# Two linear-attention and two windowed-attention layers on one core: rows of the second linear layer normalised earlier, more buffers in a preparation, transpositions spread out, and a value tile moved in attention's first segment

## The chip, the cores and the metric

The kernel runs on one core of a Trainium2 chip. The metric is the device time of one execution in microseconds. TensorE (PE in the profile) multiplies matrices and transposes by multiplying with an identity; VectorE is DVE, ScalarE is ACT, GpSimd is POOL, and SP is the engine that issues most DMAs. Each engine works through its own queue in order.

## The reference

```python
x = A_x                                            # 2048 rows of 512 floats
x = x + A(layernorm(x)); x = x + B(layernorm(x))
x = x + A(layernorm(x)); x = x + B(layernorm(x))   # the same weights again

def A(x, wqkv, w_phi, wo):           # linear attention, 32 heads of 16
    q, k, v = heads(x @ wqkv)
    f = lambda t: concat(softmax(t @ w_phi), softmax(-(t @ w_phi)))   # 32 features
    o = f(q) @ (f(k).T @ v) / (f(q) @ sum(f(k)) + 1e-6)
    return merge(o) @ wo

def B(x, wq, wk, wv, wo, beta):      # attention in 4 segments of 512 rows, with a memory M, z
    for s in range(4):
        a_dot = softmax(q_s @ k_s.T / 4 + causal_mask) @ v_s
        a_mem = phi(q_s) @ M / (phi(q_s) @ z + 1e-6)      # phi(t) = t + 1 or exp(t)
        o_s = sigmoid(beta) * a_mem + (1 - sigmoid(beta)) * a_dot
        M, z = M + phi(k_s).T @ v_s, z + sum(phi(k_s))
    return merge(o) @ wo
```

## The kernel before, in words

Everything is fp32; where a projection needs precision, an operand is split into a high part and a remainder (names `hh`/`hl`, `oh`/`ol`, `ta`, `e`, `w`) and three matmuls replace one. ACT copies the high part out of PSUM, VectorE subtracts it for the remainder. One PSUM tag, `g`, with three buffers, takes all projections and transpositions; `lg` and `mx` (one buffer each) take the scores and the scores for the row maxima, `pv` the weighted values.

The order of each engine's instructions is the order of the Python program: every call through `dve`, `act`, `pool`, `sync` and every matmul is bound to the one before it (`Ordered`, `held`). The order is made by generators that are advanced one step at a time. While `loose` is set, an instruction keeps behind the ordered ones before it, but later ones need not keep behind it.

A linear layer has two passes. `pass1` goes over four segments of 512 rows in the order `SEGS` = 1, 2, 3, 0: rows are normalised (`norm_T`: statistics `moments`, then `guard` and `root`, `refine`, then `normal`, then `columns`, which transposes a tile of 128 rows into `hT`), then projected to k, q and v; features of k are multiplied with v into `kva`; q goes to DRAM. `go` yields some 36 steps a segment, and the list `plan` says at which steps the next segment's columns, its value tile and the statistics of the segment after it are advanced. `pass2` (144 steps) reads q back, multiplies its features with the sum, and makes the layer's output.

During the first layer's `pass1`, `prepare` runs one step to one: it loads the weights of the output projections and of attention, splits them (`act.copy` for the high part, `pool.tensor_tensor` for the rest) and stores both parts to DRAM. It does 32 quarter pieces and then 12 whole ones. `rows` keeps loads of 128 rows (`xr`) ahead, `parts` takes the tiles for the parts (`oh`, `ol`).

An attention layer is `steps`. A slot is one step k; five slots make one half group m of 4 heads; 8 m make a segment. In every slot one step of `attend` (scores, exponentials) and one of `maxima` (scores again, row maxima; it runs `LEAD` = 9 slots ahead) is done. All else is written by hand in tables: "2.3 fin ln~" means at half group 2, slot 3, `finish` and one step of the next segment's normalisation (`~`: its VectorE part one slot later). "/2" does two steps of the four. `BEFORE` is the same for the slots before 0: eight projections (q, k, v) of the first segment. `FIRST` is the table of the first segment, `GAPS` of the second and third, `LAST` and `FINAL` of the fourth. In `LAST` "v", "ln", "n" and "N" advance the next linear layer's `pass1`; what is left of it runs after attention. `aside` holds what is to be done at attention's very end.

Attention begins while `pass2` ends. `A20` steps of `pass2` are done with `opening` in between (first loads, normalisation of the first segment), then `steps` starts at slot `BEGIN` = -25 and does the rest of `pass2` (`side`) spread over the slots from `MAXIMA` to 1: in each slot until the work done, in estimated nanoseconds of TensorE, reaches its share of `LEFT`.

Of the kernel before, what the change touches and what calls it, by code (L numbers as in the profile page):

```python
# [8 lines left out]
F32R = mybir.dt.float32r  # L9
# [17 lines left out]
OT = 6  # L27
TA = 8
OO = 3
MT = 2  # L30
PV = 1
G = 3
# [2 lines left out]
LEAD = 9  # L35
FINAT = 8
PAUSE, DONE = object(), object()
LEFT = 25000
BEGIN = -25
MAXIMA = -9  # L40
A20 = 105
PREP = 3
EVERY = 2
NEXT = (3, 2, 3, 2)
SEGS = (1, 2, 3, 0)
# [2 lines left out]


FIRST = """  # L50
0.1 max k2/2       | 0.3 k2~           | 0.4 m0
1.1 max q3/2       | 1.3 fin q3~       | 1.4 t1 k3/1
2.1 max m1 k3      | 2.3 fin ln~       | 2.4 ln~ ln~
3.3 fin q0+/2      | 3.0 w
3.1 max ln~        | 3.4 q0+~ t2
4.1 max k0+/2 load | 4.3 fin k0+/1     | 4.4 k0+ m2
5.0 n              | 5.3 fin q1+/2 n
5.1 max v0+        | 5.4 q1+~ t3
6.1 max a0+ v1+    | 6.2 n             | 6.3 a0+ fin k1+/2
# [37 lines left out]
6.1 max out~       | 6.3 fin           | 6.4 pt~  # L97
7.1 p pt~          | 7.3 fin p pt      | 7.4 p pt
"""
BEFORE = {-25: "q0", -23: "v0", -21: "k0", -20: "load", -19: "v1",  # L100
          -18: "n", -17: "v2 n", -16: "n", -15: "n n", -14: "q1 n", -13: "n", -12: "k1 n", -11: "n", -10: "v3 n",
          -4: "max q2~", -1: "t0"}


# [1 line left out]
def interleave_kernel(ctx, tc, x_in, a_wqkv, a_wphi, a_wo, b_wq, b_wk, b_wv, b_wo, b_beta,  # L106
# [29 lines left out]
    aside = [None]  # L136
# [163 lines left out]
    def prepare():  # L300


        yield from constants()
        for _ in range(PREP):
            yield
        jobs = [(src, kc) for src in (b_wq, b_wk, a_wo, b_wv, b_wo) for kc in range(NC)]
        asked = []

        def rows():

            while jobs and len(asked) < 3:
                src, kc = jobs.pop(0)
                asked.append(T2("xr", 3))
                sync.dma_start(out=asked[-1], in_=src[kc * P : (kc + 1) * P, :])
            return asked.pop(0)

        def parts():
            return rows(), T2("oh", OO, F32R), T2("ol", OO, F32R)

        def pieces():  # L320
            for m in range(2):
                for kc in range(NC):
                    tiles = parts()
                    for e in range(2):
                        for r in range(2):
                            views = [tiles[0].rearrange("p (c f r e d) -> p e r c d f", c=NC, f=2, r=2, e=2)]
                            views += [t.rearrange("p (c f e d r) -> p e r c d f", c=NC, e=2, f=2, r=2)
                                      for t in tiles[1:]]
                            keep = [wqk[m][:, :, a, kc, :] for a in range(2)] if e and r else ()
                            yield [v[:, e, r] for v in views], keep, tiles[1:]  # L330
            for key in ("awo", "bwv", "bwo"):
                kept[key] = [dtile((P, NC, D), nm(key)) for _ in range(2)]
                for kc in range(NC):
                    tiles = parts()
                    yield tiles, [k[:, kc, :] for k in kept[key]], tiles[1:]

        def turn_by_turn():
            loose[0] = True
            piece = next(todo, None)
            loose[0] = False  # L340
            return piece

        copied, stored, todo = None, None, pieces()
        for piece in chain(iter(turn_by_turn, None), (None, None)):
            loose[0] = True
            if stored:
                _, keep, tiles = stored
                for k, t in zip(keep, tiles):
                    dma(k, t.rearrange("p (c x) -> p c x", c=NC) if len(k.shape) == 3 else t)
            if copied:  # L350
                (raw, hi, lo), _, _ = copied
                pool.tensor_tensor(out=lo, in0=raw, in1=hi.bitcast(F32), op=SUB)
            if piece:
                (raw, hi, _), _, _ = piece
                act.copy(hi, raw)
            loose[0] = False
            copied, stored = piece, copied
            for _ in range(EVERY):
                yield
# [131 lines left out]
        dve.tensor_tensor(out=t, in0=p[:, :, :, 0:DH], in1=rb, op=MUL)  # L491
        eng.tensor_tensor(out=out, in0=out, in1=t, op=ADD)

    def v_tile(hT, w, vv, tag):
        v = sp.tile([P, 4, VROW], F32, tag="v", bufs=2, name=nm("v"))
        vv[:] = [v]
        pool.memset(v[:, :, 0 : H * VW].rearrange("p t (h e) -> p t h e", e=VW)[:, :, :, DH : DH + 1], 1.0)
        pool.memset(v[:, :, H * VW : VROW], 0.0)
        for t in range(4):
            po = PS(*tag)  # L500
            yield from tok_proj(po, hT, t, w)
            act.copy(v[:, t, 0 : H * VW].rearrange("p (h e) -> p h e", e=VW)[:, :, 0:DH],
                           po.rearrange("p (h e) -> p h e", e=DH))
            yield
# [80 lines left out]
    class LayerA:  # L585
# [68 lines left out]
        def pass1(self, first):  # L654
            hTs, vv = [], []

            def upcoming(n):

                h = []
                spare = ("e8" if first else "w8") if n % 2 else None  # L660
                return h, norm_T(self.xsrc, SEGS[n], h, spare, slow=True, off=True)

            if first:
                wq, wk, wv, upc = self.first(hTs, vv, upcoming)
            else:
# [9 lines left out]
                    next(vt)  # L675
                    yield
                wk = load_w("awk", None, "e8")
                yield from vt
            self.mmq = [T2("mmq", 2, shape=(P, NT // 2, 2, H)) for _ in range(2)]
            kva = sp.tile([P, 8, 4 * VW], F32, tag="acc", bufs=1, name=nm("kva"))  # L680
            late = None
            for n, s in enumerate(SEGS):
# [53 lines left out]
                    yield  # L736

                if n < NSEG - 1:
                    if n == 0 and not first:
                        upc = upcoming(1)  # L740
                        next(upc[1])
                    hTs, g = upc
                    vv = []
                    if n or first:
                        plan = [(4 + j, g) for j in range(4)]
                        vals, norms = [10 + j * 26 // 16 for j in range(16)], (8, 14, 16, 18, 20, 22, 24, 28, 30, 32, 34)
                    else:
                        plan = [(j, g) for j in (8, 9, 12, 13, 14, 15, 17, 18, 19, 20)]
                        vals, norms = [21 + j * 13 // 16 for j in range(16)], (21, 26, 27, 28, 29, 30, 31, 33, 34, 35, 36)
                    vt = v_tile(hTs, wv, vv, ("g", G))  # L750
                    plan += [(j, vt) for j in vals]
                    if n + 2 < NSEG:
# [24 lines left out]
                    for i, _ in enumerate(go(late)):  # L777
                        if i == 4 and n == 0 and not first:
                            wq = load_w("awq", None, "e8")
                            aside[0].append(lambda: [next(g) for _ in range(4)])  # L780
                        while plan and plan[0][0] <= i:
                            next(plan.pop(0)[1], None)
                        if n == 1 and i % 4 == 0:
                            settle(1)
                        yield
# [84 lines left out]
    class LayerB:  # L870
# [20 lines left out]
        def values(self, s):  # L891

            self.vv[s] = []
            yield from v_tile(self.hT[s], self.wv, self.vv[s], ("g", G))

        def queue_w(self):

# [395 lines left out]
    for i in range(2):  # L1293
# [3 lines left out]
        opening = lb.opening()  # L1297
        for k in range(A20):
            next(a2)
            if k in (6, 9, 12, 18, 24, 30) or k > 41 and k % 3 == 0:  # L1300
                next(opening, None)
        for _ in opening:
            pass
# [32 lines left out]
```

## Time and profile before

| | us |
|---|---|
| median of three runs | 1599.54 |
| lowest and highest | 1596.80, 1601.78 |
| the profiled execution | 1604.31 |
| its span, first to last instruction | 1602.6 |
| busy: PE / DVE / ACT / POOL | 1518.1 / 1130.9 / 785.6 / 651.7 |
| mean granted TensorE clock | 0.983 |

The profile is of one execution. A line of the timeline has the start, the busy time, the engine, the operation with output and inputs, the count of merged instructions, and in brackets the idle time of the engine before it and what ended that. An idle time is a loss only where the engine is the one that sets the pace; here this is TensorE for nearly all of the span. Names of tiles are without buffer numbers; `x` is rows, `st` their statistics, `P` the exponentials or features, `mxs` the maxima. Line 183 is the helper of all matmuls, 187 that of all transpositions, 161 that of all other engines, so lines say little here, and one goes by tiles.

### The profile page before, as it was taken

Reading aid. Unit: us, or ns where it says so; the run is one execution under the profiler, and the core shown is the slowest. Engines: PE = TensorE matmul, PEld = TensorE weight load, DVE = VectorE, ACT = ScalarE, POOL = GpSimd, SP = SyncE. Lnnn points to the kernel's source line nnn. Section 1 sums busy time; section 2 is a strip of 40 time slices with the busy share of each in tenths; the row PEclk is TensorE's granted clock in tenths of the full one; section 3 lists DMA queues with packets and bytes.
Section 4 is the critical chain, followed back from the end, with each engine's and each line's share of the span. In section 5 each row is a group of like instructions: output and inputs, shape, how many; then the busy total and the mean of one; then the engine's idle time right before and its main releaser. Section 6 shows DMA issues by size and latency. Waiting matters only on the chain.

```text
span 1602.6 us, 28186 instructions
## 1 busy us (share of the span) xinstructions
PE 1518.1 (95%) x9856; PEld 1083.3 (68%) x9856; DVE 1130.9 (71%) x3252; ACT 785.6 (49%) x1178; POOL 651.7 (41%) x1006
## 2 busy tenths in 40 slices
PE   7998999988999999999989999998989999999997
PEld 6787887765566666665557888877556666666554
DVE  5654677577778878878554557756788788787783
ACT  5543345325565565565533323343455655655553
POOL 1567555213444544433222336532234444433322
PEclk9998999999999999999988999999999999999999
DMA  4477265534443543535231103735353444444331
GB/s 161 135 260 256 66 198 158 157 99 134 126 112 104 143 99 105 142 94 152 90 129 40 40 20 101 235 105 147 111 170 110 107 136 103 106 112 101 80 102 39
DMA packets 108765, 195.71 MB, mean 122 GB/s; under 512 B 14416, under 2 KB 27856, under 8 KB 107856
## 3 DMA queue, kind: packets, MB, share of 16 engines
q1 hardware_dynamic: 107472, 193.38, 41.2%
q8 instruction: 79, 1.29, 0.4%
q10 hardware_dynamic: 1152, 0.52, 0.1%
q14 instruction: 62, 0.51, 0.1%
HBM read 101.05 MB, written 39.85 MB: 88 GB/s over the span
## 4 chain that ended last, share of the span: by engine, by line
PE 67%; DVE 18%; ACT 5%; issue 5%; POOL 3%; DMA 2%; SPq 0%; ACTq 0%; POOLq 0%; DVEq 0%
PE g L183 38%; DVE mx L161 8%; PE lg L183 8%; PE mx L183 8%; PE g L187 7%; PE pv L183 7%; POOL P L161 2%; ACT tb L161 2%; DVE es L161 2%; ACT P L161 1%; DVE mxs L161 1%; DVE ta L161 1%; DVE mmq L161 1%; ACT x L161 1%; DMA xr<-in 1%
## 5 line engine op out<-in xcount | busy, mean ns | idle before, releaser
L161 DVE CUSTOM_DVE_ANT_0 mx<-mx,mask 128x128 f32<-128x128 f32 (+3 forms) x1024 | 510.9, 499 | 163.2 <-PE mx L183 128.6
L161 ACT ACTIVATE P<-lg 128x1024 f32<-128x1024 f32 x320 | 328.8, 1028 | 178.9 <-PE lg L183 171.1
L161 POOL TENSOR_SCALAR_AFFINE_SELECT P<-P 128x256 f32<-128x256 f32 (+1 forms) x448 | 191.3, 442 | 444.3 <-ACT P L161 443.2
L183 PE MATMUL g<-hh,wqk 128*128 128x512 f32 x512 | 180.3, 407 | 1.0 <-ACT mt L161 0.7
L183 PE MATMUL mx<-e,e 63*128 63x256 f32 (+2 forms) x1024 | 156.2, 362 | 25.8 <-DVE mxs L161 20.2
L183 PE MATMUL lg<-e,e 64*128 64x256 f32 (+2 forms) x1024 | 168.5, 387 | 7.9 <-ACT P L161 7.1
L183 PE MATMUL g<-w,oh 128*128 128x512 f32 x512 | 171.5, 417 | 4.3 <-DVE hl L161 2.5
L183 PE MATMUL pv<-P,v 128*32 128x512 f32 (+3 forms) x2048 | 166.1, 443 | 0.0
L183 PEld LDWEIGHTS lg<-e,e 64*128 64x128 f32 x1024 | 81.2, 184 | 102.7 <-issue 53.9
L183 PE MATMUL g<-w,hh 128*128 128x512 f32 x448 | 145.5, 406 | 1.5 <-ACT tb L161 0.9
L161 DVE DVE_READ_ACCUMULATOR2_ANT mxs<- 128x1 f32 x1024 | 144.8, 141 | 0.0
L183 PEld LDWEIGHTS mx<-e,e 63*128 63x128 f32 x1024 | 83.2, 186 | 74.8 <-DVE mxs L161 55.9
L183 PEld LDWEIGHTS pv<-P,v 128*32 128x32 f32 x2048 | 54.0, 110 | 99.6 <-issue 89.2
L183 PEld LDWEIGHTS g<-hh,wqk 128*128 128x128 f32 x512 | 96.3, 188 | 22.3 <-ACT mt L161 1.1
L183 PEld LDWEIGHTS g<-w,oh 128*128 128x128 f32 x512 | 90.9, 192 | 27.3 <-issue 2.8
L161 POOL TENSOR_SCALAR tb<-tb 128x512 f32<-128x512 f32 x48 | 71.5, 1491 | 82.0 <-ACT tb L161 82.0
L183 PE MATMUL g<-w,ol 128*128 128x512 f32 x256 | 103.0, 402 | 0.0
L183 PE MATMUL g<-hl,wqk 128*128 128x512 f32 x256 | 100.0, 390 | 0.0
L161 ACT COPY v<-g 128x512 f32<-128x512 f32 x64 | 37.6, 587 | 120.1 <-PE g L183 119.8
L161 ACT CAST ta<-g 128x512 fp32r<-128x512 f32 x64 | 37.5, 585 | 117.4 <-PE g L183 117.4
L183 PEld LDWEIGHTS g<-w,hh 128*128 128x128 f32 x448 | 79.8, 189 | 20.3 <-ACT tb L161 2.7
L183 PE MATMUL g<-w,hl 128*128 128x512 f32 x224 | 88.1, 393 | 0.0
(133 smaller groups left out, 2729.5 us busy)
## 6 DMA issues: line engine op xcount, KB each, us to landing
e<-ta SPq DMA_DIRECT2D x384, 128.0 KB
wqk<-wqk SPq DMA_DIRECT2D x64, 512.0 KB
x<-x SPq DMA_DIRECT2D x48, 256.0 KB
xr<-in SPq DMA_DIRECT2D x28, 256.0 KB
pq<-tb SPq DMA_DIRECT2D x24, 256.0 KB
tb<-pq SPq DMA_DIRECT2D x24, 256.0 KB
x<-xr SPq DMA_DIRECT2D x24, 256.0 KB
xr<-x SPq DMA_DIRECT2D x24, 256.0 KB
```

Of the source, the lines that this page charges most:

```text
L161: i = f(*a, **k)
L183: return held(nc.tensor.matmul(*a, **k))
L187: return held(nc.tensor.transpose(*a))
```

## The change

Five things change. In `prepare` up to five row loads run ahead instead of three, into the six buffers `ot` instead of the three of `xr`, and both parts come from the eight buffers `ta1` instead of three each of `oh` and `ol`. In `pass1` of the second linear layer the normalisation of the second segment is begun while the value tiles of the first are projected (in attention's last rows), with its refinement on VectorE instead of GpSimd, and its last steps follow early in the first segment; the steps done at attention's end fall away. In all other segments of `pass1` columns and statistics come at other steps, further apart. At attention's start five more steps of `pass2` come before the slots, the rest begins at slot -14 instead of -9, and the list `STEPS` replaces a rule for when `opening` is advanced. In attention's first segment the last value tile moves behind slot 0, the value tiles are made in the order 0, 3, 1, 2 (in every segment), the product m0 comes a slot later, and the four transposition steps "ln" stand in four slots instead of three.

```diff
-LEFT = 25000
+LEFT = 21700
 BEGIN = -25
-MAXIMA = -9
-A20 = 105
+MAXIMA = -14
+STEPS = (6, 9, 12, 18, 24, 30, *range(42, 91, 3), 93, 100, 102, 109)
+A20 = 110
...
 FIRST = """
-0.1 max k2/2       | 0.3 k2~           | 0.4 m0
-1.1 max q3/2       | 1.3 fin q3~       | 1.4 t1 k3/1
-2.1 max m1 k3      | 2.3 fin ln~       | 2.4 ln~ ln~
-3.3 fin q0+/2      | 3.0 w
-3.1 max ln~        | 3.4 q0+~ t2
-4.1 max k0+/2 load | 4.3 fin k0+/1     | 4.4 k0+ m2
+0.1 max k2/2       | 0.2 v3/2          | 0.3 k2~
+0.4 v3             | 1.1 max m0 q3/2   | 1.3 fin q3~       | 1.4 t1 k3/1
+2.1 max m1 k3      | 2.3 fin ln~       | 2.4 ln~
+3.1 max ln~        | 3.3 fin ln~       | 3.0 w
+3.4 q0+/2 t2       | 4.1 max q0+~ load | 4.3 fin k0+/2     | 4.4 k0+ m2
...
-BEFORE = {-25: "q0", -23: "v0", -21: "k0", -20: "load", -19: "v1",
-          -18: "n", -17: "v2 n", -16: "n", -15: "n n", -14: "q1 n", -13: "n", -12: "k1 n", -11: "n", -10: "v3 n",
+BEFORE = {-25: "q0", -23: "v0", -21: "k0", -20: "load",
+          -18: "n", -17: "v1 n", -16: "n", -15: "n n", -14: "q1 n", -13: "n", -12: "k1 n", -11: "n", -10: "v2 n",
           -4: "max q2~", -1: "t0"}
...
-            while jobs and len(asked) < 3:
+            while jobs and len(asked) < 5:
                 src, kc = jobs.pop(0)
-                asked.append(T2("xr", 3))
+                asked.append(T2("ot", OT))
...
-            return rows(), T2("oh", OO, F32R), T2("ol", OO, F32R)
+            return rows(), T2("ta1", TA, F32R), T2("ta1", TA, F32R)
...
-    def v_tile(hT, w, vv, tag):
+    def v_tile(hT, w, vv, tag, order=range(4)):
...
-        for t in range(4):
+        for t in order:
...
-            def upcoming(n):
+            def upcoming(n, off=True):
...
-                return h, norm_T(self.xsrc, SEGS[n], h, spare, slow=True, off=True)
+                return h, norm_T(self.xsrc, SEGS[n], h, spare, slow=True, off=off)
...
                 wk = load_w("awk", None, "e8")
-                yield from vt
+                upc = upcoming(1, False)
+                next(upc[1])
+                for n, _ in enumerate(vt):
+                    if n > 1:
+                        next(upc[1])
+                    yield
...
-                    if n == 0 and not first:
-                        upc = upcoming(1)
-                        next(upc[1])
                     hTs, g = upc
                     vv = []
-                    if n or first:
-                        plan = [(4 + j, g) for j in range(4)]
-                        vals, norms = [10 + j * 26 // 16 for j in range(16)], (8, 14, 16, 18, 20, 22, 24, 28, 30, 32, 34)
-                    else:
-                        plan = [(j, g) for j in (8, 9, 12, 13, 14, 15, 17, 18, 19, 20)]
-                        vals, norms = [21 + j * 13 // 16 for j in range(16)], (21, 26, 27, 28, 29, 30, 31, 33, 34, 35, 36)
+                    plan = [(j, g) for j in ((0, 2, 4, 4, 8, 9, 11, 13) if n == 0 and not first else (4, 7, 10, 13))]
+                    vals, norms = [10 + j * 26 // 16 for j in range(16)], (14, 20, 22, 24, 26, 27, 28, 31, 33, 34, 35)
...
                             wq = load_w("awq", None, "e8")
-                            aside[0].append(lambda: [next(g) for _ in range(4)])
...
-            yield from v_tile(self.hT[s], self.wv, self.vv[s], ("g", G))
+            yield from v_tile(self.hT[s], self.wv, self.vv[s], ("g", G), (0, 3, 1, 2))
...
-            if k in (6, 9, 12, 18, 24, 30) or k > 41 and k % 3 == 0:
+            if k in STEPS:
                 next(opening, None)
```

## The prediction

> **What bounds the kernel now.** I read the page's slices first, then busy time by windows, then the timeline and the chain of waits where the windows show loss.
>
> ```profile
> PE   7998999988999999999989999998989999999997
> PEclk9998999999999999999988999999999999999999
> 147.39:151.48 4.09, 0.00 (x0) 0.00 (x0) 4.02 (x7) 1.45 (x4) 2.02 (x3) 0.82 0.92 302
> 150.02:160.26 10.24, 8.78 (x36) 8.29 (x37) 2.39 (x4) 1.24 (x2) 7.12 (x6) 0.50 0.66 246
> 832.68:853.16 20.48, 16.86 (x63) 14.45 (x64) 8.82 (x14) 6.12 (x10) 5.51 (x7) 0.50 0.22 64
> 281.88:305.20 23.32, 23.16 (x107) 18.72 (x105) 7.33 (x15) 7.80 (x15) 4.04 (x8) 1.00 0.60 176
> 305.20:352.40 47.20, 42.77 (x233) 32.42 (x232) 36.39 (x109) 15.20 (x25) 8.79 (x9) 0.93 0.38 109
> 352.40:400.70 48.30, 41.57 (x314) 24.99 (x313) 37.79 (x131) 26.89 (x37) 18.10 (x34) 1.00 0.46 132
> ```
>
> (Columns of a window: length; busy PE, PEld, DVE, ACT, POOL; PE clock; DMA share; GB/s.) TensorE is busy 95% of the span and the change alters no matmul, so it can win only idle TensorE time (1602.6 − 1518.1 = 84.5 us) and stretches at half clock. The loss sits where the change works: the weight preparation in the first pass (slice at 120–160), the passage from the first attention layer to the second linear layer (820–880), and the start of each attention layer (305–400; the second, 1093–1190, shows the same waits).
>
> ```profile
> 145.64 0.62 ACT L161 CAST oh<-xr 128x512 fp32r<-128x512 f32 x1 [3.62 <-DMA bwv<-ol]
> 146.49 1.29 POOL L161 TENSOR_TENSOR ol<-xr,oh 128x512 fp32r<-128x512 f32 x1 [0.95 <-DMA bwv<-ol]
> 151.48 6.67 PE L183 MATMUL lg<-v,P 128*128 128x68 f32 x30 [4.09 <-POOL P L161]
> ...
> 832.56 0.70 POOL L161 TENSOR_SCALAR st<-st 128x4 f32<-128x4 f32 x1
> 833.29 2.93 ACT L161 ACTIVATE x<-x,st 128x512 f32<-128x512 f32 x4 [1.03 <-POOL st L161]
> 834.16 1.11 PE L187 MATMUL g<-ident,x 128*128 128x128 f32 x4 [4.12 <-ACT x L161]
> 841.09 1.12 PE L187 MATMUL g<-ident,x 128*128 128x128 f32 x4 [1.96 <-DVE w L161]
> ```
>
> First stall: the preparation's cast sits 3.62 us at the head of ACT's queue waiting on a DMA, the copies behind it reach VectorE late, and TensorE waits 4.09 us for scaled features. Second: rows normalised too late hold TensorE 4.12 and 1.96 us. A half-clock stretch follows each.
>
> **The change, part by part** (minus is a gain).
>
> *More buffers in prepare().* Casts, subtractions and stores stay; five row loads instead of three run ahead, in six buffers instead of three, and four pairs of parts instead of three. The cast at 145.64 needed a row loaded, or a part stored, about 5 us before (the store issued at 140.96 lands at 146.34); pieces come 2.4 us apart, so one or two more pieces of lead cover most of it. On SP a load no longer stands until the subtraction just before it frees its buffer (SP waited 29.2 us for `ol` between 60 and 290); two loads more at the start, 0.5 MB, fall into the slice with DMA share 0.4. Worth: 4.09 idle, plus half of the 8.78 us busy in the half-clock stretch, 4.39: 8.5. Against it: DMA share is 0.92 there, and the last 12 pieces move 9.4 MB in about 36 us, 260 GB/s, where the busiest windows reach 390. Bounds 0 and −8.5; nearer the full amount: **−7.5**.
>
> *Transpositions apart in pass 1.* Columns at steps 4, 7, 10, 13 instead of 4 to 7; waits before such transposes are 1.06 (at 42.39), 1.56 (127.12), 0.97 and 1.59 (876.70, 879.64), 0.95 (923.93): 6.1. Each is a VectorE remainder or an ACT copy behind other work of the same step; three steps (some 4 us) between them should clear half. The later loads (step 14 rather than 8) still stand six steps ahead of their statistics. Bounds −6 and +1: **−3**.
>
> *Second linear layer's rows sooner.* Gain: statistics, root and the refinement (now on VectorE) come before the end of attention. 4.12 + 0.19 + 1.95 idle go, and half of the 16.86 us busy in the half-clock stretch, 8.4: −14.7. Cost: where the statistics are moved to. They stand in VectorE's program at slots 6.3 and 6.4 of the last attention segment, some 790 us, ahead of the weighing of the memory product and of the early projection's remainder `ol`. Their rows come through SP, whose queue there reads
>
> ```profile
> 791.55 0.32 SPq L161 DMA_DIRECT2D tb<-x  x1
> 791.92 3.83 SPq L161 DMA_DIRECT2D e<-awk  x8
> 795.84 2.46 SPq L161 DMA_DIRECT2D x<-x  x4
> 796.00:799.00 3.00, 3.00 (x14) 2.45 (x15) 0.69 (x1) 1.03 (x1) 0.41 (x1) 1.00 0.94 240
> 799.00:802.00 3.00, 3.00 (x30) 1.55 (x28) 0.56 (x1) 2.23 (x4) 0.41 (x2) 1.00 1.04 393
> 802.00:805.00 3.00, 2.71 (x15) 2.19 (x14) 0.68 (x2) 1.29 (x2) 1.83 (x4) 1.00 0.58 214
> ```
>
> The row loads keep their place behind 2 MB of awk, itself behind a load that waited 21.5 us for TensorE; the DMA engines work that off until about 804, so row 0 lands near 802. VectorE, in order, stands from 790.5 until then. Behind it wait the weighing that frees one of three g buffers and the `ol` that the matmul at 795.86 uses third. Statistics cost 0.87 us a row: two rows and 0.9 us of weighing, TensorE goes on at 804.3; two more rows and the 0.56 us `ol`, 806.8. So it idles about 8.4 + 2.1 = 10.5 us it does not idle now; queued behind it are all projections of slot 7.1 on. After idle times of 4 us the trace shows half clock for 10.24 and 20.48 us, elsewhere for 3.41; two windows of 3.41 with TensorE busy cost 3.4. Net −14.7 + 13.9: **−1**; bounds −14.7 (rows there in time) and +4 (three windows, and a microsecond or two for ACT's root before VectorE's refinement). The refinement's six small operations, 0.2 us each, leave POOL for VectorE. The four normalisations (0.80 us each on ACT) and four moments otherwise lie beside work: ACT and VectorE have idle times of 1 to 3 us in every slot there.
>
> The Trainium skill (TensorE: Matmul & The Clock Gate, "What's actually happening") says that one busy window of about 3.4 us restores the full clock; by it the new stall would cost 1.7 instead of 3.4 us of clock, and this term be about −2.5. The trace disagrees for the two stretches of 10.24 and 20.48 us, three and six windows, with TensorE busy 82 to 86% of them.
>
> *Attention's start* (twice). The list STEPS gives the same 24 useful calls as the old rule (up to 93; the later three find the opening finished): nothing. Five steps of pass 2 run before the slots: four transposes 0.60, two products 2.24, half an output projection 1.38: 4.2 us. The rest is spread over 16 slots from −14 instead of 11 from −9, so 5/16 of 21.7 = 6.8 us falls among the projections; a value tile (2.75 us; eight projections take 22.0) leaves them. The dense stage gets +4.2 + 6.8 − 2.75 = +8.2, at full clock. The stage of first maxima (305.20 to 352.40) loses 11.0 us of TensorE work and some 8 us of VectorE's (4.4 us a tile: remainder 0.69, scaling 1.75, weighing 1.3, residual 0.69). Its floors, TensorE 42.77 − 3.4 (two half-clock windows) and VectorE 36.39, then fall to 28.4 each; its slack over the higher floor, 7.8 us, will grow as TensorE's matmuls and VectorE's maxima share one mx buffer and alternate: 38 us, −9.2. Bounds: no saving at all, and −13. The value tile comes back at slots 2 and 4, into gaps of 0.93 + 0.24 + 0.61 + 0.87 us: +1 (0.1 to 2.75). If that cover goes, the whole 2.75 is paid. The memory product, a slot later, has its reader in the next segment. The value order (0, 3, 1, 2) asks for tiles 0 and 3 first, as the weighted product does: nothing. The ln transpositions of segment 0: the gaps from 382 to 393 (3.3 us) lose perhaps 0.5. Per start 8.2 − 9.2 + 1 − 0.5 = −0.5: **−1** for two, bounds −10 and +17.
>
> Sum: −7.5 − 3 − 1 − 1 = −12.5. The profiled execution took 1604.31 (span 1602.6 and 1.7 around it), so 1591.8 in its terms; it stands 4.8 above the median 1599.54, so the median after is **1587.0**.
>
> **The rivals.**
>
> *The rows come in time*: were they loaded before VectorE reaches the statistics, 13.9 us of new stall vanish and the time is 1573. For it: a normalisation asked for earlier is what the edit says. Against it: SP's lines above; nothing ahead of the rows leaves the queue.
>
> *The DMA wait only moves in prepare()*: at 0.92 share more loads in flight make each slower, another cast stops, and the part is worth 0 to −1: 1594. For it: the share; against it: 0.2 to 0.3 of the engines in use between 106 and 117, room to load ahead.
>
> *Slower: the first maxima keep their length.* If the 47.2 us are set by the alternation over the one mx buffer (11 slots of 4.3 us, VectorE busy 77%) and not by the side work, the saving of 9.2 fails and both starts cost 8.2 + 1 − 0.5 = 8.7, together +17.4: −11.5 + 17.4 = +6, 1605.5. It decides from a saving below 3.4 us per start. For it: seven of its eight gaps over 0.2 us are waits on VectorE or ACT. Against it: from 352 to 401 the slots take 2.7 us with the same maxima, so 4.3 is not their own pace.
>
> **How the numbers follow.** About 0.3%, 4.8 us, is what a measurement of this kernel can tell from no change: faster is below 1594.7, slower above 1604.3. Forecast 0.45 (own range 1579 to 1595), rows in time 0.17, DMA wait moved 0.20, maxima keep their length 0.18. Faster: 0.43 + 0.17 + 0.09 = 0.69; same: 0.02 + 0.11 + 0.03 = 0.16; slower: 0.15. The range leaves out the best half of the first rival and the end of the last: 1570 to 1603.
>
> **What would show it.** Right: no cast waiting on a DMA near 145 and no half clock near 150–160; no TensorE gap before the first transposes after attention and no 20.48 us half clock there; in its place a gap of about 10 us before an early `g<-w,oh`, with VectorE's first BATCH_NORM behind `DMA x<-x`; first maxima in about 38 us, the projections before them in about 31. Wrong: that gap absent (1573); PE idle on POOL's P or on DMA in 120–160 as now; the stage of first maxima above 44 us; a new half clock after it.

## The result: 25 us slower, and the profile after

| | before | after |
|---|---|---|
| median in one comparison, us | 1601.78 | 1626.60 |
| lowest and highest, us | 1596.80, 1604.25 | 1625.62, 1632.32 |
| the profiled execution (its span), us | 1604.31 (1602.6) | 1628.92 (1627.2) |
| mean granted TensorE clock | 0.983 | 0.976 |

The ratio is 1.0171, 95% interval 1.0151 to 1.0191: slower, above the predicted range. The page's slices of the changed kernel show it only faintly:

```profile
PE   7998999898999999999789999998989999999997
PEclk9999999889999999999989999998989999999999
```

The fourth clock digit (the preparation) is back at 9; new dips stand at the eighth and ninth clock digits (start of the first attention layer), at the twentieth PE digit (its end), and at the twenty-eighth and thirtieth clock digits (start of the second). The positions of the same matmuls in both timelines give the ledger, in us of the two profiled executions:

| stretch, by its first and last matmul | before | after | change |
|---|---|---|---|
| start to pass 2's first `g<-KN,P` | 208.12 | 206.67 | -1.5 |
| to the first maxima `mx<-e,e` | 97.1 | 115.1 | +18.0 |
| to the first scores `lg<-e,e` | 39.1 | 30.1 | -8.9 |
| to the first `pv<-P,v` | 16.5 | 15.1 | -1.4 |
| first segment, to its seventh group of `pv<-P,v` | 40.6 | 45.7 | +5.1 |
| from there to the last scores | 405.4 | 418.5 | +13.1 |
| passage and second linear layer, to `g<-KN,P` | 189.5 | 178.8 | -10.7 |
| second start: to `mx`; to `lg`; to `pv` | 97.1; 38.9; 16.5 | 113.2; 28.9; 15.2 | +16.1; -10.0; -1.3 |
| first segment there, to the seventh group | 40.6 | 46.8 | +6.2 |
| the rest of the span | 413.2 | 413.0 | -0.2 |

So five places lose (both starts, both first segments, the end of the first attention layer) and the passage, the stages of maxima and the first pass gain. By windows, with the columns of the prediction's windows: the first stage of maxima up to the first scores, before and then after, and in the last line the stretch at attention's end:

```profile
305.20:344.27 39.07, 34.64 (x194) 26.85 (x193) 30.63 (x94) 11.90 (x20) 7.98 (x7) 0.91 0.40 115
```
```profile
321.81:351.95 30.14, 25.61 (x132) 18.32 (x132) 22.09 (x74) 5.59 (x11) 1.05 (x1) 0.83 0.31 88
809.05:822.70 13.65, 4.95 (x11) 3.45 (x12) 4.88 (x14) 0.42 (x2) 0.00 (x0) 0.51 0.40 143
```

POOL's and VectorE's side work has left the stage of maxima and it is 9 us shorter, as forecast. In the last line TensorE is busy for 4.95 of 13.65 us. The timeline there, of SP, VectorE and TensorE:

```profile
802.74 4.86 SPq L161 DMA_DIRECT2D e<-awk  x8
807.64 3.01 SPq L161 DMA_DIRECT2D x<-x  x4
814.13 0.69 DVE L161 BATCH_NORM_STATS2 bs<-x 128x6 f32<-128x512 f32 x1 [12.85 <-DMA x<-x]
818.37 0.55 DVE L161 TENSOR_TENSOR ol<-g,oh 128x384 fp32r<-128x384 f32 x1
816.70 1.22 PE L183 MATMUL g<-w,oh 128*128 128x512 f32 x2 [9.95 <-DVE tmp L161]
818.97 0.79 PE L183 MATMUL g<-w,ol 128*128 128x512 f32 x1 [1.05 <-DVE ol L161]
853.48 1.46 PE L183 MATMUL g<-w,w 128*128 128x512 f32 x3 [2.95 <-DVE w L161]
```

The rows' loads stand behind awk on SP; VectorE waits 12.85 us at the first statistics; TensorE waits 9.95 us for the weighing queued behind them and 1.05 for the remainder behind the next two. This is the stall of the prediction, to half a microsecond. The last line is what is left in the passage of the 4.12 and 1.95 us before.

The start of the first attention layer, which was not foreseen; the first two lines are the kernel before, the others the changed kernel:

```profile
296.05 0.69 DVE L161 BATCH_NORM_STATS2 bs<-x 128x6 f32<-128x512 f32 x1 [3.04 <-DMA x<-x]
298.11 0.69 DVE L161 BATCH_NORM_STATS2 bs<-x 128x6 f32<-128x512 f32 x1 [1.15 <-DMA x<-x]
```
```profile
291.33 5.77 SPq L161 DMA_DIRECT2D wqk<-wqk  x2
297.20 1.81 SPq L161 DMA_DIRECT2D x<-x  x4
301.21 0.70 DVE L161 BATCH_NORM_STATS2 bs<-x 128x6 f32<-128x512 f32 x1 [3.11 <-DMA x<-x]
303.81 0.69 DVE L161 BATCH_NORM_STATS2 bs<-x 128x6 f32<-128x512 f32 x1 [1.70 <-DMA x<-x]
306.68 0.68 DVE L161 TENSOR_TENSOR xr<-g,xr 128x512 f32<-128x512 f32 x1
307.41 0.98 PE L187 MATMUL g<-ident,P 128*128 128x128 f32 x4 [3.40 <-DVE xr L161]
1108.60 0.65 PE L187 MATMUL g<-ident,P 128*128 128x128 f32 x4 [2.75 <-DVE xr L161]
407.60 0.69 DVE L161 TENSOR_TENSOR hl<-g,hh 128x512 fp32r<-128x512 f32 x1
408.35 0.79 PE L183 MATMUL g<-hl,wqk 128*128 128x512 f32 x1 [2.27 <-DVE hl L161]
```

The second segment's rows (`x<-x`) leave SP at 297.20, behind 5.77 us of `wqk`. VectorE stands for them, 3.11 and 1.70 us, and has all four statistics to do before pass 2's addition `xr`, for which TensorE waits 3.40 us (2.75 in the second layer). In the kernel before VectorE stands for the same rows, and TensorE does not wait. The last two lines are the first segment's new wait, on the remainder `hl` (2.28 us at 1209.74 in the second layer). TensorE is granted half its clock for 53 us of the execution before and 77 of the one after: such stretches stand at each of these waits (from 307.60 and from 406.58 for 6.83 us, from 809.36 for 13.65), and from 328.08 for 10.24 in the maxima.

### The profile page after: what moved, and what is told of

It is laid out like the page before. It is cut to its first block, busy times and chain, and to the rows that moved or that the text cites. A ratio compares the mean times of both kernels' runs of the same rounds, so it can differ in the third digit from the quotient of the medians.

```text
span 1627.2 us, 28180 instructions
## 1 busy us (share of the span) xinstructions
PE 1525.7 (94%) x9856; PEld 1084.1 (67%) x9856; DVE 1132.3 (70%) x3258; ACT 785.7 (48%) x1178; POOL 649.7 (40%) x1000
## 4 chain that ended last, share of the span: by engine, by line
PE 68%; DVE 16%; ACT 6%; issue 4%; POOL 3%; DMA 2%; SPq 1%; DVEq 0%; POOLq 0%; ACTq 0%
PE g L183 39%; PE lg L183 8%; PE mx L183 8%; DVE mx L161 8%; PE pv L183 7%; PE g L187 7%; POOL P L161 2%; ACT P L161 2%; ACT tb L161 2%; DVE es L161 1%; DVE mxs L161 1%; DMA x<-x 1%; DVE ta L161 1%; SPq L161 1%; DVE mmq L161 1%
## 5 line engine op out<-in xcount | busy, mean ns | idle before, releaser
L183 PE MATMUL g<-hh,wqk 128*128 128x512 f32 x512 | 184.6, 416 | 2.1 <-ACT hh L161 1.4
```

The lines of the kernel that those rows point to most:

```text
L183: return held(nc.tensor.matmul(*a, **k))
```

## The experiments

Theory after the result: each part that slows the kernel has put work behind a VectorE wait that was already there or that it makes itself (late rows; a group of maxima), at a place where TensorE's next matmul needs that work. The rival: the moves cost by their own amount (TensorE or VectorE simply has more to do in the dense stretch). Each kernel below is the kernel before with the edit named, if not said otherwise; times are medians against the kernel before in the same comparison.

**One part at a time.** *Second linear layer's rows sooner* (all of that part's edits in `pass1`):

```diff
+                upc = upcoming(1, False)
+                next(upc[1])
...
-                            aside[0].append(lambda: [next(g) for _ in range(4)])
```

> The kernel before with one part alone: the second linear layer's rows of its second segment normalised in attention's last slots, refinement on VectorE. Theory (rows late): the row loads stand behind awk on SP, VectorE waits for them and TensorE idles about 10 us before an early g<-w,oh, with some 13 us at half clock behind it, +13.7 by the slots' times of after; the passage to the next pass 2 gains 10.7 and the last half clock before it 1.3. Sum +2, between -1 and +4. Rival (the stall in after comes from another part of the change, which shifted the slots): no gap before g<-w,oh, and -12 to -14.

1605.28 against 1601.09, ratio 1.0029 (1.0012 to 1.0047). TensorE waits 9.93 us on `tmp` and 1.06 on `ol` at 793 to 806, half clock from 797 for 13.65 us, and from the last scores to pass 2 it takes 177.3 instead of 189.5 us. The whole stall and the whole gain belong to this part.

*Attention's start* (spread of pass 2 and value tile together, with the tiles' order and m0, and the old rule for the opening), then *with STEPS as well*:

```diff
-LEFT = 25000
+LEFT = 21700
-MAXIMA = -9
+MAXIMA = -14
-A20 = 105
+A20 = 110
...
-BEFORE = {-25: "q0", -23: "v0", -21: "k0", -20: "load", -19: "v1",
-          -18: "n", -17: "v2 n", -16: "n", -15: "n n", -14: "q1 n", -13: "n", -12: "k1 n", -11: "n", -10: "v3 n",
+BEFORE = {-25: "q0", -23: "v0", -21: "k0", -20: "load",
+          -18: "n", -17: "v1 n", -16: "n", -15: "n n", -14: "q1 n", -13: "n", -12: "k1 n", -11: "n", -10: "v2 n",
```

> The kernel before with the start of attention alone: five more steps of pass 2 first, the rest from slot -14 on, last value tile behind slot 0, tiles in the order 0, 3, 1, 2; the opening's steps by the old rule and the ln transpositions as before. Theory (VectorE's statistics of the second segment's rows wait for their DMA, and what pass 2 now has on VectorE stands behind them): a TensorE gap of about 3 us near 304 and 1106 on DVE xr and half clock after it, 6.5 us each; with +8.2 for the denser projections and -10.3 for the shorter stage up to the first weighted values, +4 to +5 a start, +9 in all. Rival (the loss of after's starts comes from the opening's last transposition at step 109 and from the ln transpositions): no such gap, -2 a start, -4 in all.

> The spread start (five more steps of pass 2, rest from slot -14, value tile moved) with the new list STEPS as well, so that it differs from the run with the spread start alone by the list only. The prediction called the list without effect; in after the opening's last transposition stands at step 109, right before the first projection, with waits of 0.7, 0.7 and 0.2 us and a half-clock stretch of 3.4 us. Theory: +2 to +3 for each start over the spread start alone, +4 to +6 in all, so +18 to +20 on the kernel before. Rival (prediction): the same as the spread start alone, +14.5.

1615.62 against 1601.09, ratio 1.0103 (1.0074 to 1.0132): the largest loss of all parts. TensorE waits 3.33 and 2.59 us on `xr`. With STEPS 1617.93 against 1600.92, 1.0104 (1.0077 to 1.0130): nothing that can be told apart, where 4 to 6 us more were expected.

*First segment's transpositions and projections* (the "ln" and "q0+" entries of `FIRST`):

```diff
-2.1 max m1 k3      | 2.3 fin ln~       | 2.4 ln~ ln~
-3.3 fin q0+/2      | 3.0 w
-3.1 max ln~        | 3.4 q0+~ t2
-4.1 max k0+/2 load | 4.3 fin k0+/1     | 4.4 k0+ m2
+2.1 max m1 k3      | 2.3 fin ln~       | 2.4 ln~
+3.1 max ln~        | 3.3 fin ln~       | 3.0 w
+3.4 q0+/2 t2       | 4.1 max q0+~ load | 4.3 fin k0+/2     | 4.4 k0+ m2
```

> The kernel before with the ln transpositions of attention's first segment in four slots instead of three and the projections behind them moved. Theory (the first projection of the next segment now follows one slot after the last transposition, and its third matmul waits for a remainder that stands behind a group of maxima on VectorE): a gap of about 2.3 us on DVE hl in each layer and 3 to 7 us of half clock behind it, +4.5 us each, +9 in all. Rival (the gap in after is a result of the shifted value tile): no gap on DVE hl, within 1 us of before each, 0 to -2 in all.

1609.54 against 1601.09, ratio 1.0059 (1.0040 to 1.0078); waits of 2.28 and 2.27 us on `hl` and three new half clocks of 3.41 us. In the trace the two first segments are 4.9 and 2.8 us longer, 7.7 of the 8.5.

*Preparation*:

```diff
-            while jobs and len(asked) < 3:
+            while jobs and len(asked) < 5:
...
-            return rows(), T2("oh", OO, F32R), T2("ol", OO, F32R)
+            return rows(), T2("ta1", TA, F32R), T2("ta1", TA, F32R)
```

> The kernel before with the preparation's buffers alone (five row loads ahead in six buffers, four pairs of parts). Theory: the 4.09 us gap near 147 and its half clock go, 8.5 us; after shows 1.1 to 3.3 us of new waits on POOL's P and VectorE between 128 and 150 and 3.4 us of half clock at the end of pass 1 (198 to 205), where the matmuls are 68 wide; -3 to -5 if that half clock comes with it, -6 to -8 if not. Rival (the wait on DMA only moves): 0 to -1, casts or subtractions of ACT and POOL waiting on DMA as before.

1597.55 against 1601.09, ratio 0.9976 (0.9957 to 0.9995). In its trace the stall near 147 and the half clock after it are gone and pass 2 begins at 198.8 instead of 208.1; other half clocks, of 6.8 us at 893 among them, give back part.

*Columns and normalisations of pass 1* (all but the second linear layer's first segment):

```diff
-                        plan = [(4 + j, g) for j in range(4)]
-                        vals, norms = [10 + j * 26 // 16 for j in range(16)], (8, 14, 16, 18, 20, 22, 24, 28, 30, 32, 34)
+                        plan = [(j, g) for j in (4, 7, 10, 13)]
+                        vals, norms = [10 + j * 26 // 16 for j in range(16)], (14, 20, 22, 24, 26, 27, 28, 31, 33, 34, 35)
```

> The kernel before with one part alone: in pass 1's other segments the transposed columns at steps 4, 7, 10, 13 and the later statistics. Theory (what the prediction had as -3 is a loss): comparing after with the kernel that has the new preparation alone, pass 2 begins 6 us later, 3.4 of it half clock, and in the second linear layer 1.5 later than with the earlier rows alone; here +1.5 to +7, the waits before single transpositions replaced by waits of the same size elsewhere (ACT tb, POOL P). Rival (the prediction): -3, the waits of 1.06, 1.55 and 1.59 us gone and none in their place.

1608.79 against 1600.92, ratio 1.0039 (1.0017 to 1.0062). The waits of 1.06, 1.56 and 1.59 before transposes are gone, as forecast, and others stand before one transpose and before the products of features and values; a half clock of 6.83 us stands beside each of the last two. These waits are on ScalarE and GpSimd, so the theory does not cover this part:

```profile
123.81 0.66 PE L187 MATMUL g<-ident,x 128*128 128x128 f32 x4 [1.00 <-ACT tb L161]
877.09 4.44 PE L183 MATMUL mx<-v,P 128*128 128x68 f32 x30 [1.05 <-POOL P L161]
925.18 4.72 PE L183 MATMUL mx<-v,P 128*128 128x68 f32 x30 [1.09 <-POOL P L161]
```

**Taking the late loads away.** *Rows sooner, with their loads issued one step of the value tiles earlier*, ahead of the `tb` load and of awk on SP:

```diff
-                for _ in range(8):
+                for i in range(8):
                     next(vt)
+                    if i == 7:
+                        upc = upcoming(1, False)
+                        next(upc[1])
                     yield
```

> The earlier normalisation alone, its four row loads asked for one value step sooner, so that on SP they stand ahead of the early projection's loads and of awk. Theory (VectorE stood for the rows): no gap before g<-w,oh near 795, no 13.7 us at half clock, and the gain of the passage stays: -10 to -13 on the kernel before, 14 to 17 below the earlier rows alone. Rival (the statistics in those slots, or the refinement on VectorE, are the cost, whenever the rows come): a gap of several us stays, 0 to +4.

1588.85 against 1600.92, ratio 0.9922 (0.9895 to 0.9948). No wait before the early projections and no half clock there; VectorE's statistics start at 788.53 without a wait. The order of two groups of loads on SP turns +4.2 into -12.1.

*Attention's start (spread and value tile), with the second segment's rows loaded five slots earlier*:

```diff
-BEFORE = {-25: "q0", -23: "v0", -21: "k0", -20: "load",
+BEFORE = {-25: "load q0", -23: "v0", -21: "k0",
```

> The spread start with the loads of the second segment's rows before the first projection (slot -25 instead of -20), ahead of the weight tiles on SP. Theory (the rows' DMA holds VectorE and with it pass 2's additions): VectorE's statistics near 300 wait for no DMA, the gaps of 3.3 and 2.6 us on DVE xr and the half clock behind the first go; about 9 us below the spread start alone, +3 to +6 on the kernel before. Rival (the denser stage itself costs what was measured): the same as the spread start alone within 3 us.

1606.04 against 1600.92, ratio 1.0028 (1.0014 to 1.0042): the wait on `xr` is gone and some 9.5 us of the 14.5 with it. Up to its first maxima each start is 9.5 us longer than in the kernel before, where the kernel with late loads had 16.2 and 12.2. 5 us of the median remain.

*The whole change with these two loads earlier, and nothing else*:

> The changed kernel with nothing but its two groups of row loads moved: the second linear layer's one value step sooner, attention's second segment's from slot -25 instead of -20. Theory (the late rows hold VectorE in both places and make most of the loss): no gap of 10 us before g<-w,oh and none on DVE xr; 16 + 9.5 us below the changed kernel, 1600 to 1604. Rival (what the parts cost singly was an effect of their being single): 1612 or more.

1597.66 against 1602.38, ratio 0.9980 (0.9964 to 0.9997): 29 us below the changed kernel. The waits on `hl` remain.

**What the start's cost is made of.** *Value tile, its order and m0 alone* (with the edit of `BEFORE` above), and *the spread alone*:

```diff
-0.1 max k2/2       | 0.3 k2~           | 0.4 m0
-1.1 max q3/2       | 1.3 fin q3~       | 1.4 t1 k3/1
+0.1 max k2/2       | 0.2 v3/2          | 0.3 k2~
+0.4 v3             | 1.1 max m0 q3/2   | 1.3 fin q3~       | 1.4 t1 k3/1
...
-            yield from v_tile(self.hT[s], self.wv, self.vv[s], ("g", G))
+            yield from v_tile(self.hT[s], self.wv, self.vv[s], ("g", G), (0, 3, 1, 2))
```
```diff
-LEFT = 25000
+LEFT = 21700
-MAXIMA = -9
+MAXIMA = -14
-A20 = 105
+A20 = 110
```

> The kernel before with the value tile alone moved behind slot 0, the order 0, 3, 1, 2 and the product m0 a slot later; pass 2's rest and the opening as before. The spread start with its loads first still cost 2 to 7 us, of which the times of the weighted values show 2.2 per start within the first segment's first six slots, at a wait of 1.36 us on ACT's P. Theory (the tile's matmuls crowd slots 2 to 6): +1 to +2 per start after the first weighted values, less 1 to 2 before them, 0 to +3 in all. Rival (pass 2's spreading causes it): those slots as before, -1 to -3 in all.

> Only LEFT, MAXIMA and A20 are changed: pass 2 is spread over the slots from -14, the value tile stays in the opening. With the value tile moved as well the whole cost 14.5 us, the value tile alone 6.9. Theory (two separate causes, both lost cover: pass 2's additions queue on VectorE behind the statistics of the second segment's rows, whose loads are late; and without the value projection nothing hides ScalarE's copies): here about 7 of the 14.5 us are left, 1606 to 1609, with a gap before g<-ident,P on DVE xr of 2 to 3.5 us at both starts and a half clock after at least one of them, and no 3 us gap on ACT tb. Rival (the gap on xr comes from the value tile's move too, since the statistics come earlier by a projection): no gap on xr above 1.5 us, 1597 to 1602.

Value tile: 1609.23 against 1602.38, ratio 1.0054 (1.0038 to 1.0071), more than the 0 to +3 expected. Spread: 1605.28 against 1600.91, 1.0027 (1.0015 to 1.0039). The first lines are the value tile's kernel (VectorE, ScalarE, TensorE), the next the kernel before at the same product, the last the spread's:

```profile
296.21 0.69 DVE L161 BATCH_NORM_STATS2 bs<-x 128x6 f32<-128x512 f32 x1 [3.08 <-DMA x<-x]
301.79 0.45 ACT L161 ACTIVATE st<-st 128x4 f32<-128x4 f32 x2 [6.66 <-DVE st L161]
307.19 1.16 PE L183 MATMUL g<-KN,P 128*128 128x68 f32 x8 [3.05 <-ACT tb L161]
```
```profile
306.63 1.11 PE L183 MATMUL g<-KN,P 128*128 128x68 f32 x8 [0.29 <-ACT tb L161]
```
```profile
300.91 0.69 DVE L161 BATCH_NORM_STATS2 bs<-x 128x6 f32<-128x512 f32 x1 [3.37 <-DMA x<-x]
304.76 0.68 DVE L161 TENSOR_TENSOR xr<-g,xr 128x512 f32<-128x512 f32 x1
305.67 1.04 PE L187 MATMUL g<-ident,P 128*128 128x128 f32 x8
```

The product's inputs come about as late as before (307.19 against 306.63), behind the same wait for rows: ScalarE, whose copy `tb` the product reads, first stands for VectorE's statistics `st`. But TensorE arrives a value projection, 2.75 us, sooner and waits 3.05 instead of 0.29. In the spread's kernel VectorE waits for the first rows just as long (3.37) and `xr` still stands behind the four statistics (304.76), yet TensorE does not wait: the value projection is still there to do. The wait on `xr` needs both edits. That refutes what I had expected of the spread alone (a wait of 2 to 3.5 us). What the spread costs by itself is hardly in the trace: dense stage +12.3, maxima -10.4, then -1.5, so 0.4 us at the first start (0.9 at the second); the timed 4.4 is more, and that remainder is not explained. It may lie in the executions and not in the start: the kernel before was profiled in one of 1604.31, which is 3.4 above its median here, and no trace shows what its faster executions save.

*The spread alone with the earlier loads* (both edits as above):

> The spread of the kernel above, with the second segment's rows loaded five slots earlier, ahead of the first projection. Theory: no gap on DVE xr, the first maxima take 36 to 40 us instead of 47, the projections before them some 7 to 10 us longer, so the starts come out 0 to 2 us to the good each: 1596 to 1601. Rival (spreading pass 2 over more slots costs by itself, since its waits fall among projections that fill TensorE): weighted values begin 2 us or more later at each start, 1603 to 1607.

1605.99 against 1600.91, ratio 1.0030 (1.0018 to 1.0042). That is the rival's time, though the weighted values begin less than 1 us later at each start. Early loads give nothing where the projection hides the wait. With the spread and early loads, then, the value tile's move is free (1.0028 with it, 1.0030 without). The value tile alone with early loads was not run.

*The "ln" steps apart but with the old lead*, projections as before:

```diff
-2.1 max m1 k3      | 2.3 fin ln~       | 2.4 ln~ ln~
-3.3 fin q0+/2      | 3.0 w
+2.1 max m1 k3      | 2.3 fin ln~       | 2.4 ln~
+3.3 fin q0+/2      | 3.0 w ln~
```

> The kernel before with the four ln transpositions in four slots as the change has it, but ending at slot 3.1 (2.3, 2.4, 3.0, 3.1) with the projections where they were. Theory (what the change's ln edit costs is the short lead of the last transposition before the projection that reads it, not the spreading): no wait on DVE hl near 397, -1 to +1. Rival (single transpositions in slots that VectorE sets are the cost): +4 to +8.

1601.59 against 1602.38, ratio 1.0009 (0.9990 to 1.0028), no wait on `hl`. Four slots instead of three cost and gain nothing. What is left of the part is the later last transposition (3.3 instead of 3.1), one slot before the projection that reads it (3.4), and the later projections; the wait on `hl` puts the 8.5 us on the lost lead.

**Columns and normalisations taken apart.** *Columns at 4, 7, 10, 13 with the old normalisations*, and *the changed kernel with only the normalisations put back*:

```diff
-                        plan = [(4 + j, g) for j in range(4)]
+                        plan = [(j, g) for j in (4, 7, 10, 13)]
```

> Only the steps of the columns in pass 1 are changed (4, 7, 10, 13 instead of 4 to 7), in all segments but the second linear layer's first; the statistics and normalisations keep their old steps. With both changed the time rose by 6 to 8 us, all in the second linear layer. Theory (the later normalisations and loads cost: they fall into the last ten steps beside the scaling of features on GpSimd and ScalarE): 1597 to 1602, passage and second layer within 1.5 us of the kernel before, no new half clock beside kv matmuls. Rival (the columns in later steps push the kv products' features back): 1605 to 1609, with the waits of 1.05 and 1.09 on POOL P and half clocks in the second layer again.

> The changed kernel whole, with only the normalisations of pass 1 put back to their old steps (8 to 34) in all segments but the second linear layer's first; columns stay at 4, 7, 10, 13. Theory (the later normalisations are what cost in the columns' part: 9 us between the two kernels that differ in them alone): 1626.6 falls to 1617 to 1621. Rival (their cost hung on the late rows in the passage, which the changed kernel treats otherwise): 1624 to 1628.

Columns alone: 1597.90 against 1600.91, ratio 0.9977 (0.9964 to 0.9990), so -3.0. With the later normalisations the same columns cost 8. The expected absence of new half clocks beside the products did not come true: a wait of 1.06 us on `P` at 871.79 and 6.83 us of half clock stand there with the old normalisations too; the second such pair, at 925 to 934, is missing. In the changed kernel the old normalisations bring 1624.50 (ratio 1.0140, 1.0119 to 1.0162) against its 1626.60 (1.0171, 1.0151 to 1.0191): 2 to 5 us, not 9, and as the intervals overlap it may be nothing. The later normalisations' cost depends on what is around them.

**The best version.** *More buffers in the preparation, and rows sooner with early loads; start, first segment and columns as before*:

> The kernel before with the two parts that gained: the preparation's buffers, and the earlier normalisation with its row loads one value step sooner. Attention's start, the ln transpositions and the columns as before. If the parts add up: -3.5 - 12.1, -14 to -18 on the kernel before, neither the 4 us gap on POOL's P near 147 nor one before the first transposes after attention. Rival (what is won early is lost to half-clock stretches elsewhere): -9 to -12.

**1584.44 against 1602.38, ratio 0.9889 (0.9869 to 0.9909)**: below both kernels. In the passage only this wait is left (the trace is of its slowest execution, 1592.02):

```profile
826.18 1.33 PE L183 MATMUL g<-w,w 128*128 128x512 f32 x3 [2.96 <-DVE w L161]
```

*The same with the spread and the second segment's loads first*, and *the same with the columns apart, old normalisations*:

> The best kernel so far (more buffers in the preparation, second linear layer's rows sooner with their loads one value step earlier; 1584.4) with the spread of pass 2 and the second segment's rows loaded first. If the spread with early loads gains, 1580 to 1584; if it is worth nothing, 1583 to 1586; if it costs by itself, 1588 to 1592.

> The best kernel so far (more buffers in the preparation, second linear layer's rows sooner with their loads one value step earlier; 1584.4) with the columns of pass 1 at steps 4, 7, 10, 13 and the normalisations at their old steps, which alone gave 3 us. Theory (the columns' gain lies in waits on VectorE and ScalarE before transposes, the buffers' in the preparation's stall): part of the 3 us was the stall near 147, which the buffers have taken already, so 1581 to 1584. Rival (all of it was that stall, or a half clock that came one window shorter): 1584 to 1587.

1587.76 against 1600.91 (0.9906, 0.9882 to 0.9931) and 1587.89 against 1603.28 (0.9916, 0.9899 to 0.9932): neither adds anything. In the second, the preparation's stall is back in spite of the buffers, and none of its waits is for a DMA (ACT, VectorE, POOL, TensorE):

```profile
141.96 0.62 ACT L161 CAST ta<-ot 128x512 fp32r<-128x512 f32 x1 [2.76 <-POOL P L161]
143.09 1.28 DVE L161 TENSOR_REDUCE mmq<-tb 128x32 f32<-128x512 f32 x2 [2.10 <-ACT tb L161]
146.16 1.58 POOL L161 TENSOR_TENSOR P<-P,es 128x512 f32<-128x512 f32 x1 [1.72 <-DVE es L161]
147.79 6.67 PE L183 MATMUL lg<-v,P 128*128 128x68 f32 x30 [3.15 <-POOL P L161]
```

The cast waits for GpSimd, the `tb` copy behind it keeps VectorE waiting, VectorE's sum `es` keeps GpSimd waiting, and the features come late: a ring of three queues. The columns' steps and the preparation's steps meet here, and the two parts do not add.

## Why the prediction was wrong, point by point

The sum was -12.5 and the change cost +24.8. Three terms that were put at nothing or at a gain are losses: the starts, the columns, and ln with q0+.

| term | predicted, us | measured alone, us |
|---|---|---|
| buffers | -7.5 | -3.5 (9.3 in its own trace up to pass 2) |
| columns (with later normalisations) | -3 | +7.9 (columns without them -3.0) |
| rows sooner | -1 | +4.2 |
| starts, STEPS included | 0 | +14.5 to +17 |
| ln and q0+ | -1 | +8.5 |
| sum | -12.5 | +32 to +34; the whole +24.8 |

*Rows sooner: right in mechanism, 5 us off in size.* Forecast: TensorE idle 10.5 us behind the rows' DMA; measured 9.95 + 1.05. Of half clock, TensorE was busy 4.95 us in the 13.65, so about 2.5 lost where 3.4 was forecast. By the rule of the Trainium skill that the prediction weighed (TensorE: Matmul & The Clock Gate, "What's actually happening") the loss would be an estimated 1.7. The trace shows full clock 6.3 us after the first matmul at 816.70; but the wait of 1.05 us lies in the first half of these, and the last 3.4 are without a wait, so this stretch does not speak against one busy window. The stretch of 6.83 us at 198.37, with TensorE busy for all of it, does. The return was 10.7 to 12.2 us instead of 14.7: a wait of 2.95 on the remainder `w` stays. The rival "rows in time" was priced at 13.9 below; the kernel with early loads measured 16.3 below the one without.

*Maxima: right.* The prediction's stage, which ends two slots after the first scores, took 36.8 and 35.5 us instead of 47.2 and 47.1: -10.5 and -11.5 against -9.2, so the slower rival (the stage keeps its length) is refuted. Its threshold does not follow from its own sum: −11.5 + 2 × (8.7 − s) is zero at a saving s of 2.95 us, not 3.4.

*Dense stage before the maxima: the step that failed.* "The dense stage gets +4.2 + 6.8 − 2.75 = +8.2, at full clock"; it got +18.0 and +16.1. I counted TensorE's work rightly (+9.5 with early loads) and took VectorE's queue there as free. The trace of before has VectorE waiting for the same rows, 3.04 us at 296.05 and 1.15 at 298.11; it cost nothing because what stood behind the statistics was needed later than the value projection ended. The change removes that projection and puts pass 2's additions into that queue: 3.40 us of wait, then half clocks of 6.83 us there and 10.24 in the maxima. With the start's edits alone the late rows cost 16.2 − 9.5 = 6.7 us at the first start (3.33 of wait and half of 6.83 at half clock) and 12.2 − 9.5 = 2.7 at the second (2.59 of wait). The prediction named the cover of the value tile's new place (its gaps), but not that the tile's old place was itself a cover. So the tile's +1, bounded by 2.75, measured 6.9 for two starts, 3.4 each.

*STEPS: misread, at no cost that can be measured.* The opening needs 27 steps, not 24: in the changed kernel its last column is asked for at step 109 (remainder 0.23 us late at 286.93), so the later three did not "find the opening finished". A half clock of 3.41 us follows there at 287.12; the kernel with the start and STEPS alone has none.

*ln and q0+: the wait moved from transposition to projection.* The part named the gaps it would close (3.3 us) but not the lead it took away: q0+ asks one slot after the last transposition, and VectorE's remainder `hl` stands in that slot behind a group of row maxima. 2.27 us, and as much again in half clock.

*Columns: the sign was wrong as made, right for the columns.* "Should clear half" of 6.1 us: the columns alone gave 3.0, with the later normalisations they lost 7.9. The sentence that failed says of the later loads that they "still stand six steps ahead of their statistics": it looked at the loads, not at what the normalisations meet in steps 20 to 35. Of the some 10 us between the two traces 2.9 lie before pass 2, 2.0 in the first maxima, which neither edit touches, and 5.0 in the passage and the second linear layer (a wait of 1.09 and 6.83 us of half clock more). Which queue causes them is not settled.

*Buffers: right in mechanism, half in size.* The stall and its half clock went, as forecast. In the changed kernel the first linear layer is only 1.5 us shorter: the first load came 1.1 us later, its columns bring waits of 1.01, 1.34, 0.88 and 1.14, and a half clock of 6.83 us stands at 198.37. The rival (the DMA wait only moves) did not happen; that a ring of queues takes its place was seen in the best kernel with columns.

## What to carry to other kernels

Before moving work off a place, ask what it was hiding there: an idle time of a non-critical engine that costs nothing today is a debt, due when work is queued behind it or the cover in front of its reader goes. When an engine is to read sooner, move the DMA first and look at what stands ahead of it on the issuing queue; here moving two groups of loads was worth 29 us in the changed kernel, more than the whole change had cost. Do such parts one by one: their sum here was off by 7 to 9 us, and two that gain alone (buffers, columns) did not gain together in the best kernel.

## What was not expected of the hardware

Half clock comes in stretches of 3.41 us and its multiples (3.41, 6.83, 10.24, 13.65, 20.48) in every trace, apart from one cut short by the end of the execution, and not only after waits of several us: in the changed kernel one starts at 198.37 with TensorE busy for all its 6.83 us, 2.5 us after a wait of 0.73. Two kernels with the same first linear layer (buffers alone, and buffers with rows sooner) differ there by such a stretch: none in the one execution, 6.8 us at 195 in the other, with pass 2 beginning at 198.8 and 203.5. The buffers' kernel was timed from 1593.1 to 1605.8. So terms of 3 us can be read from a trace only as waits; what the clock makes of them differs from execution to execution.
